# Pairing the 64-row remainder of a contraction in the two row halves of TensorE, and writing a bias to PSUM from ScalarE

## The chip, the cores and the metric

The kernel runs on one core of a Trainium2 chip. The metric is device time in microseconds (us) of one execution, the median of several. A profile's "span", from the first to the last instruction, is 1.4 to 2.1 us shorter than that time. The "granted clock" is the share of its full clock that TensorE was given, as a mean over the run unless a stretch is named. PSUM is the memory, in banks, in which TensorE's matmuls add up their sums; an "eviction" is the instruction of another engine that reads a finished sum out of it. The profile names the engines PE (TensorE matmul), PEld (TensorE weight load), DVE (VectorE), ACT (ScalarE), POOL (GpSimd) and SP (SyncE, which issues transfers). "L525" is line 525 of the kernel that is profiled, so the same code has other line numbers in other kernels.

## The reference, cut to what matters

```python
g = sigmoid((x * gate_w).sum(-1, keepdims=True))      # x: 2048 rows, 640 features
a = ssm(x, ...)                                       # complex recurrence, then y = 2 Re(h C) + x * Dskip
h = gelu(x @ w1 + b1)                                 # 640 -> 1728 features
b = h @ w2 + b2                                       # 1728 -> 640
out = g * a + (1 - g) * b
```

1728 = 13 x 128 + 64. The second linear layer, `h @ w2 + b2`, contracts over 13 full blocks of 128 features and a remainder of 64. The change is about that remainder and about `b2`.

## The kernel before

The 2048 rows are worked off in four chunks of 512 rows (four row tiles of 128). For each chunk there are four kinds of matmul work: `ssm` (input of the recurrence), `ff1` (first linear layer, with GELU on ScalarE), `fin_b` (second linear layer) and `fin_a` (output of the recurrence, C matrix). Their order is:

```python
    # ... ff1(0) ...
    ssm(0); ff1(1); ssm(1)
    for ks in range(KS):
        fold(ks)                 # scale the C matrix once, on ScalarE and VectorE
    fin_b(0); fin_a(0)
    ssm(2); ff1(2); fin_b(1); fin_a(1)
    ssm(3); ff1(3); fin_b(2); fin_a(2)
    fin_b(3); fin_a(3)           # (cut: gates, loads)
```

The second linear layer, and the scaling of C:

```python
    def fin_b(c):
        for a in range(TPC):                               # 4 row tiles (cut: ti and lo, the tile's number and first row)
            gb = fwork.tile([P, D], F32, name="gb")
            if a >= TPC - 2:
                seed(c * TPC + a - (TPC - 2))              # VectorE writes x * Dskip to PSUM for fin_a
            for d0, d1 in HALVES:                          # (0, 320), (320, 640)
                p = bank()
                for kf in range(KF):                       # 14: 13 full blocks and the remainder
                    m = P if kf < KF - 1 else F_LAST + 1   # 65 rows: 64 features and a row of ones for b2
                    nc.tensor.matmul(p[:, 0:d1 - d0], lhsT=gel[c][:m, kf, lo:lo + P], rhs=w2_sb[:m, kf, d0:d1],
                                     start=(kf == 0), stop=(kf == KF - 1))
                nc.scalar.activation(out=gb[:, d0:d1], in_=p[:, 0:d1 - d0], func=ACT.Identity, scale=gcol[:, 1, ti:ti + 1])

    def fold(ks):
        t1 = fwork.tile([P, D], F32, name="gb")
        t2 = fwork.tile([P, D], F32, name="gb")
        # ScalarE: t1 = CT_im * n2im ; t2 = CT_re * n2im
        # VectorE: CT_re = CT_re * c2re + t1 ; CT_im = CT_im * n2re + t2
```

In the timelines below, each engine starts its matmuls or evictions in the order in which the kernel issues them (ScalarE at the end of `ff1(2)`: L271 at 108.79, L295 at 109.46, L297 at 109.74). With `start=True` the first matmul of a group replaces what the bank held, so `fin_b` needs no value from another engine in its banks before it begins, and the trace of before has no wait of TensorE at its line, L525.

## Time and profile before

| | before |
|---|---|
| device time, median of 3 | 217.63 us (217.43 to 217.79) |
| span of the profiled run | 216.2 us |
| TensorE / VectorE / ScalarE busy | 98% / 88% / 42% |
| `fin_b` per chunk | 15.25 us, 112 matmuls of 320 columns, 136 ns each |

First the busy table of the page (engine, busy us, share of the span, instructions).

```profile
PE 211.9 (98%) x1368; PEld 128.2 (59%) x1368; DVE 189.8 (88%) x393; ACT 91.7 (42%) x156; POOL 1.6 (1%) x12
```

Then the chain of waits, in order of time (start us, length us, what, how many). This is the work that ended last, followed back from the end. From 22.5 us to the last matmul it is all matmuls; five of its pieces are shown: L267 is `ff1`, L525 `fin_b`, L544 `fin_a`.

```profile
57.81 15.25 PE bank L525 x112
73.06 10.87 PE bank L544 x80
94.72 14.03 PE bank L267 x65
109.36 15.24 PE bank L525 x112
202.27 10.91 PE bank L544 x90
```

Two unit costs can be read from it. 65 matmuls of 512 columns in 14.03 us make 215.8 ns each, 112 of 320 columns in 15.25 us make 136 ns each. A matmul's own duration in the profile is longer (299 ns for 320 columns) than the 136 ns from one start to the next, so the records of neighbours overlap: use this pitch, not the duration.

The timeline where `ff1(2)` ends and `fin_b(1)` begins (start us, length us, engine, line, operation). L292 is the small tile of the last 64 GELU features.

```profile
108.58 0.78 PE L292 MATMUL bank<-w1b,xT 128*128 128x65 bf16 x20
108.79 0.69 ACT L271 ACTIVATE gel<-bank,colB 128x512 bf16<-128x512 f32 x1 [0.39 <-PE bank L267]
109.20 0.57 PE L525 MATMUL bank<-w_sb,gel 128*128 128x320 bf16 x3
109.46 0.38 ACT L295 ACTIVATE gelN<-bank 128x256 bf16<-128x256 f32 x1
109.74 0.17 ACT L297 ACTIVATE gz<-bank 128x4 f32<-128x4 f32 x1
```

TensorE starts `fin_b` at 109.20, while ScalarE still has three evictions ahead of it. TensorE does not wait for them: the list of waits has only this one of TensorE, near the start of the kernel.

```profile
PE bank L196 <- DVE halfpi L191: 1.2, 1, 1.2
```

The first and the last VectorE instruction of the folding of C:

```profile
59.91 0.88 DVE L403 SCALAR_TENSOR_TENSOR CT_re<-CT_re,c2re,gb 128x640 bf16<-128x640 bf16 x1 [0.56 <-ACT gb L399]
67.08 0.88 DVE L403 SCALAR_TENSOR_TENSOR CT_im<-CT_im,n2re,gb 128x640 bf16<-128x640 bf16 x1
```

C is ready at 68 us, and `fin_a(0)` starts at 72.9.

### The profile page before, as it was taken

The numbers are of one execution on the slowest core, as the hardware profiler recorded it, in microseconds if no ns is written. First come the engines' busy times: TensorE is split into PE (matmuls) and PEld (weight loads), VectorE is DVE, ScalarE is ACT, GpSimd is POOL, SyncE is SP. The second block draws the span as 40 slices with busy tenths as digits, with TensorE's granted clock in tenths as the row PEclk, the third lists the DMA queues.
The fourth block names the chain that finished last, engine by engine and source line by source line (L and its number), as shares of the span: only waits on it lengthen the run. The fifth ranks groups of instructions, "written<-read, shape, count | busy, mean of one in ns | idle before, by whom it ended". The sixth has DMA issues, their size and how long they took to land.

```text
span 216.2 us, 3470 instructions
## 1 busy us (share of the span) xinstructions
PE 211.9 (98%) x1368; PEld 128.2 (59%) x1368; DVE 189.8 (88%) x393; ACT 91.7 (42%) x156; POOL 1.6 (1%) x12
## 2 busy tenths in 40 slices
PE   7999999999999999999999999999999999999994
PEld 3855444454577775444477777444457777777773
DVE  3889999999999899999999999999999999961152
ACT  3689456675696101556642200456662210022100
POOL 2000000000000000000000000000000000000000
PEclk9999999999999999999999999999999999999999
DMA  5999999995000042000010006100001000100011
GB/s 174 255 224 199 226 214 369 175 246 103 3 0 0 0 141 106 0 0 3 0 24 3 0 0 200 45 2 0 0 3 24 0 3 30 61 30 3 2 61 61
DMA packets 32339, 16.16 MB, mean 75 GB/s; under 512 B 25091, under 2 KB 32324, under 8 KB 32324
## 3 DMA queue, kind: packets, MB, share of 16 engines
q1 hardware_dynamic: 32114, 15.91, 30.2%
q8 instruction: 10, 0.16, 0.3%
q10 hardware_dynamic: 210, 0.04, 0.1%
q14 instruction: 5, 0.04, 0.1%
HBM read 7.24 MB, written 2.62 MB: 46 GB/s over the span
## 4 chain that ended last, share of the span: by engine, by line
PE 88%; SPq 5%; DMA 5%; issue 0%; DVE 0%
PE bank L525 28%; PE bank L544 20%; PE bank L478 20%; PE bank L267 19%; DMA BT_im<-in_A_B_im_dram 3%; SPq L139 3%; DMA xn<-in_A_x_dram 1%; SPq L127 1%; SPq L125 1%; PE bank L292 1%; SPq L124 0%; SPq L138 0%; DVE ot L549 0%
## 5 line engine op out<-in xcount | busy, mean ns | idle before, releaser
L525 PE MATMUL bank<-w_sb,gel 128*128 128x320 bf16 x448 | 61.6, 299 | 0.0
L525 PEld LDWEIGHTS <-gel 128*128 128x128 bf16 x448 | 43.6, 98 | 17.2
L481 ACT ACTIVATE bu<-bank 128x512 bf16<-128x512 f32 x40 | 23.9, 597 | 41.7 <-PE bank L478 41.7
L271 ACT ACTIVATE gel<-bank,colB 128x512 bf16<-128x512 f32 x52 | 34.6, 693 | 15.1 <-PE bank L267 14.8
L544 PEld LDWEIGHTS <-hs 128*128 128x128 bf16 x330 | 31.8, 98 | 11.9
L434 DVE TENSOR_TENSOR_SCAN g<-r_c,carry,v 128x512 bf16<-128x512 f32 x30 | 37.2, 1270 | 0.0
L528 ACT ACTIVATE gb<-bank,gcol 128x320 f32<-128x320 f32 x32 | 16.5, 527 | 48.2 <-PE bank L525 46.6
L267 PE MATMUL bank<-xT,w1b 128*128 128x512 bf16 x140 | 31.0, 379 | 0.0
L267 PE MATMUL bank<-xT,w1a 128*128 128x512 bf16 (+1 forms) x150 | 27.6, 344 | 0.0
L544 PE MATMUL bank<-CT_im,hs 128*128 128x320 bf16 (+2 forms) x165 | 27.1, 295 | 0.0
L544 PE MATMUL bank<-CT_re,hs 128*128 128x320 bf16 (+2 forms) x165 | 27.1, 295 | 0.0
L549 DVE SCALAR_TENSOR_TENSOR ot<-bank,gcol,gb 128x320 bf16<-128x320 f32 (+2 forms) x33 | 17.3, 533 | 9.5 <-PE bank L544 9.3
L478 PE MATMUL bank<-xT,BT_im 128*128 128x512 bf16 x100 | 24.9, 379 | 0.1
L478 PE MATMUL bank<-xT,BT_re 128*128 128x512 bf16 x100 | 24.8, 379 | 0.0
L267 PEld LDWEIGHTS <-w1b 128*128 128x128 bf16 x140 | 13.6, 98 | 16.3 <-DMA w1b<-in_B_w_dram 0.3
L267 PEld LDWEIGHTS <-w1a 128*128 128x128 bf16 x150 | 14.9, 100 | 11.7
L511 DVE TENSOR_TENSOR bank<-xn,Dbc 128x320 f32<-128x320 bf16 (+2 forms) x33 | 14.3, 483 | 5.8 <-ACT gb L528 5.8
L478 PEld LDWEIGHTS <-BT_im 128*128 128x128 bf16 x100 | 9.7, 98 | 12.2 <-DMA BT_im<-in_A_B_im_dram 0.6
L478 PEld LDWEIGHTS <-BT_re 128*128 128x128 bf16 x100 | 9.7, 98 | 11.0
L415 DVE TENSOR_TENSOR v<-wa,wb 128x512 bf16<-128x512 bf16 x40 | 15.2, 421 | 0.7
L415 DVE TENSOR_TENSOR wa<-TCOS,g 128x1024 bf16<-128x1024 bf16 x20 | 13.7, 686 | 0.1
L415 DVE TENSOR_TENSOR wb<-TSIN,g 128x1024 bf16<-128x1024 bf16 x20 | 13.7, 684 | 0.0
(98 smaller groups left out, 130.7 us busy)
## 6 DMA issues: line engine op xcount, KB each, us to landing
out_dram<-ot SPq DMA_DIRECT2D x15, 160.0 KB, 1.8
w_sb<-in_B_w_dram SPq DMA_DIRECT2D x1, 2080.0 KB
xn<-in_A_x_dram SPq DMA_DIRECT2D x3, 640.0 KB, 4.9
w1b<-in_B_w_dram SPq DMA_DIRECT2D x5, 240.0 KB, 4.2
w1a<-in_B_w_dram SPq DMA_DIRECT2D x5, 192.0 KB, 3.5
xn<-in_A_x_dram SPq DMA_DIRECT2D x2, 320.0 KB
Dbc<-in_A_Dskip_dram SPq DMA_DIRECT2D x1, 160.0 KB
out_dram<-ot SPq DMA_DIRECT2D x1, 128.0 KB
```

The source lines that it names most:

```text
L139: nc.sync.dma_start_transpose(out=BT_re[:], in_=A_B_re[:, :])
L267: nc.tensor.matmul(p[:, t0:t1], lhsT=w, rhs=xT[c][:, kd, t0:t1], start=(kd == 0), stop=(kd == KD - 1))
L271: nc.scalar.activation(out=gel[c][:, kf, :], in_=p[:, :], func=ACT.Gelu_apprx_tanh, bias=b1_c[:, kf:kf + 1])
L415: nc.vector.tensor_tensor(out=o, in0=a, in1=b, op=op)
L434: nc.vector.tensor_tensor_scan(s["g"][:, ri, :], r_c[:, ks:ks + 1].to_broadcast([P, CH]), s["v"][:, ri, :], init, ALU.mult, ALU.add)
L478: nc.tensor.matmul(p[:], lhsT=BT[:, kd, ks * P:(ks + 1) * P], rhs=xT[c][:, kd, :], start=(kd == 0), stop=(kd == KD - 1))
L481: nc.scalar.activation(out=bu[:, ri, :], in_=p[:], func=ACT.Identity)
L511: dve_now(ck.pe, 0.45, lambda: nc.vector.tensor_tensor(out=p[:, 0:d1 - d0], in0=xn[c][:, a, d0:d1], in1=Dbc[:, d0:d1], op=ALU.mult))
L525: nc.tensor.matmul(p[:, 0:d1 - d0], lhsT=gel[c][:m, kf, lo:lo + P], rhs=w2_sb[:m, kf, d0:d1], start=(kf == 0), stop=(kf == KF - 1))
L528: nc.scalar.activation(out=gb[:, d0:d1], in_=p[:, 0:d1 - d0], func=ACT.Identity, scale=gcol[:, 1, ti:ti + 1])
L544: nc.tensor.matmul(p[:, 0:d1 - d0], lhsT=hs[c][:, j, lo:lo + P], rhs=CT[:, j % KS, d0:d1], start=False, stop=(j == 2 * KS - 1), skip_group ...
L549: nc.vector.scalar_tensor_tensor(out=ot[:, d0:d1], in0=p[:, 0:d1 - d0], scalar=gcol[:, 0, ti:ti + 1], in1=gbs[ti][:, d0:d1], op0=ALU.mult, ...
```

## The change

The 65-row matmul takes as long as a 128-row one: `fin_b`, in which 8 of the 112 matmuls have 65 rows, runs at 136.2 ns a matmul, and `fin_a`, in which all have 128 rows and also 320 columns, at 10.87 us / 80 = 135.9 ns. The change packs the 64 remainder features of two row tiles above each other (partitions 0 to 63 and 64 to 127) and sends them through the upper and the lower half of TensorE's rows at the same time, all in one phase per chunk. That saves half of the remainder's column time. The ones row for `b2` no longer fits, so ScalarE writes `b2` to the banks beforehand and no matmul of the group clears. Tiles become 512 and 128 columns wide; the 128-column pieces of two row tiles share a bank. The five foldings of C, until now issued together before `fin_b(0)`, are spread among its tiles and get two scratch buffers of their own.

```diff
+    gelL = [const.tile([P, H, P], BF16, name=f"gelL{i}") for i in range(2)]
+    w2l = const.tile([P, D], BF16, name="w2l")        # the 64 rows of w2, twice
+    b2bc = const.tile([P, D], BF16, name="b2bc")      # b2 on every partition
@@ fold
-        t1 = fwork.tile([P, D], F32, name="gb")       # 5 buffers
-        t2 = fwork.tile([P, D], F32, name="gb")
+        t1 = fwork.tile([P, D], F32, name="ft", bufs=2)
+        t2 = fwork.tile([P, D], F32, name="ft", bufs=2)
@@ fin_b
+    MAIN, REST = (0, 512), (512, D)
+        def shared(d0, d1, n):                        # a bank that holds the bias
+            p = bank() ...
+            nc.scalar.activation(out=v, in_=src, func=ACT.Identity)
+        def full(p, col, a, d0, d1):                  # 13 full blocks, start=False
+        def half_rows():
+            for d0, d1 in (MAIN, REST):
+                for j in range(H):
+                    for h in range(2):
+                        p, col = (wide[h * H + j], 0) if d0 == 0 else (rest[h], j * dR)
+                        nc.tensor.matmul(p[:, col:col + d1 - d0], lhsT=gelL[c % 2][h * F_LAST:(h + 1) * F_LAST, j, :],
+                                         rhs=w2l[h * F_LAST:(h + 1) * F_LAST, d0:d1], start=False, stop=True, ...)
+        for h in range(2):
+            for j in range(H):
+                a = h * H + j
+                if h == 0:
+                    wide[a] = shared(*MAIN, 1)
+            # ... full tiles; after each one an entry of `between`; half_rows() after the first half
@@ order of the stages
-    for ks in range(KS):
-        fold(ks)
-    fin_b(0)
+    fin_b(0, [lambda: (fold(0), fold(1)), lambda: fold(2), lambda: fold(3), lambda: fold(4)])
```

(Cut: the smaller transpose of the remainder, evictions, buffer counts.)

More of the change, by code (lines that the diff above doesn't have):

```diff
@@ L28 @@
 TPC = CH // P
+H = TPC // 2
 HD = D // 2
@@ L69 @@
     work = ctx.enter_context(tc.tile_pool(name="work", bufs=2))
-    fwork = ctx.enter_context(tc.tile_pool(name="fwork", bufs=5))
+    fwork = ctx.enter_context(tc.tile_pool(name="fwork", bufs=4))
     def bank(dtype=F32):
@@ L80 @@
     w1b = [const.tile([P, n1b], BF16, name=f"w1b_{kd}") for kd in range(KD)]
-    w2_sb = const.tile([P, KF, D], BF16, name="w2_sb")
+    w2_sb = const.tile([P, KF - 1, D], BF16, name="w2_sb")
     BT_re = const.tile([P, KD, D], BF16, name="BT_re")
@@ L97 @@
     b1x = const.tile([P, F_LAST + 1], BF16, name="b1x")
-    gelN = [const.tile([P, TPC, P], BF16, name=f"gelN{i}") for i in range(2)]
+    gelN = [const.tile([P, H, P], BF16, name=f"gelN{i}") for i in range(2)]
+    gelL = [const.tile([P, H, P], BF16, name=f"gelL{i}") for i in range(2)]
+    w2l = const.tile([P, D], BF16, name="w2l")
+    b2bc = const.tile([P, D], BF16, name="b2bc")
     gz = const.tile([P, NT], F32, name="gz")
@@ L108 @@
     b1_c = colB[:, KS:NB]
-    H = TPC // 2
     def load_xn(c, a0=0, a1=TPC):
@@ L132 @@
     nc.gpsimd.memset(b1x[:, F_LAST:F_LAST + 1], 0.0)
-    for i in range(2):
-        nc.gpsimd.memset(gelN[i][:, :, F_LAST:P], 0.0)
-        nc.gpsimd.memset(gelN[i][:, :, F_LAST:F_LAST + 1], 1.0)
     nc.scalar.dma_start(out=prmB[KS:NB, :], in_=B_b1[0:(KF - 1) * P].rearrange("(j p) -> j p", p=P))
@@ L144 @@
     nc.sync.dma_start(out=w2_sb[:, 0:KF - 1, :], in_=B_w2[0:(KF - 1) * P, :].rearrange("(kf p) d -> p kf d", p=P))
-    nc.sync.dma_start(out=w2_sb[:F_LAST, KF - 1, :], in_=B_w2[(KF - 1) * P:F, :])
-    nc.sync.dma_start(out=w2_sb[F_LAST:F_LAST + 1, KF - 1, :], in_=B_b2.rearrange("(o d) -> o d", o=1))
+    for h in range(2):
+        nc.sync.dma_start(out=w2l[h * F_LAST:(h + 1) * F_LAST, :], in_=B_w2[(KF - 1) * P:F, :])
+    nc.sync.dma_start(out=b2bc[:], in_=B_b2.rearrange("(o d) -> o d", o=1).to_broadcast([P, D]))
     nc.sync.dma_start(out=Dbc[:], in_=A_Dskip.rearrange("(o d) -> o d", o=1).to_broadcast([P, D]))
@@ L227 @@
     nc.scalar.activation(out=r_c[:], in_=dtl[:], func=ACT.Exp)
-    scr = gelp.tile([P, KF * CH // 2], F32, name="gel")
+    scr = gelp.tile([P, (KF - 1) * CH // 2], F32, name="gel")
     HB = 2 * HC
@@ L294, in last_tile @@
                 pe(76)
-        nc.scalar.activation(out=gelN[c % 2][:, :, 0:F_LAST], in_=pv[:, :, 0:F_LAST], func=ACT.Gelu_apprx_tanh)
+        nc.scalar.activation(out=gelN[c % 2][:].rearrange("p j (h n) -> p h j n", h=2),
+                             in_=pv[:, :, 0:F_LAST].rearrange("p (h j) n -> p h j n", h=2), func=ACT.Gelu_apprx_tanh)
         act(0.45)
@@ L298, in last_tile @@
         act(0.2)
-        nc.sync.dma_start_transpose(out=gel[c][:, KF - 1, :].rearrange("p (a t) -> p a t", a=TPC),
-                                    in_=gelN[c % 2][:].rearrange("p a n -> p (a n)"))
+        nc.sync.dma_start_transpose(out=gelL[c % 2][:], in_=gelN[c % 2][:].rearrange("p a n -> p (a n)"))
     def ff1(c, k0=0):
@@ L314, in gel_tile @@
     def gel_tile(c):
-        gel[c] = gelp.tile([P, KF, CH], BF16, name="gel")
+        gel[c] = gelp.tile([P, KF - 1, CH], BF16, name="gel")
     gel_tile(0)
@@ L512, in seed @@
             seeded[ti].append(p)
-    def fin_b(c):
-        for a in range(TPC):
-            ti = c * TPC + a
-            lo = a * P
-            gb = fwork.tile([P, D], F32, name="gb")
-            if a >= TPC - 2:
-                seed(c * TPC + a - (TPC - 2))
-            for d0, d1 in HALVES:
-                p = bank()
-                for kf in range(KF):
-                    m = P if kf < KF - 1 else F_LAST + 1
-                    nc.tensor.matmul(p[:, 0:d1 - d0], lhsT=gel[c][:m, kf, lo:lo + P], rhs=w2_sb[:m, kf, d0:d1],
-                                     start=(kf == 0), stop=(kf == KF - 1))
-                    pe(d1 - d0)
-                nc.scalar.activation(out=gb[:, d0:d1], in_=p[:, 0:d1 - d0], func=ACT.Identity, scale=gcol[:, 1, ti:ti + 1])
-                act(0.5)
-            gbs[ti] = gb
+    MAIN, REST = (0, 512), (512, D)
@@ new lines, in fin_b, with out_of @@
+    def fin_b(c, between=()):
+        between = list(between)
+        wide, rest = [None] * TPC, [None] * H
+        def shared(d0, d1, n):
+            p = bank()
+            v = p[:, 0:n * (d1 - d0)]
+            src = b2bc[:, d0:d1]
+            if n > 1:
+                v = v.rearrange("p (j d) -> p j d", j=n)
+                src = src.rearrange("p (o d) -> p o d", o=1).to_broadcast([P, n, d1 - d0])
+            nc.scalar.activation(out=v, in_=src, func=ACT.Identity)
+            act(0.6 if n == 1 else 0.4)
+            return p
+        def full(p, col, a, d0, d1):
+            for kf in range(KF - 1):
+                nc.tensor.matmul(p[:, col:col + d1 - d0], lhsT=gel[c][:, kf, a * P:(a + 1) * P], rhs=w2_sb[:, kf, d0:d1],
+                                 start=False, stop=False, skip_group_check=True)
+                pe(d1 - d0)
+        def out_of(p, col, a, d0, d1):
+            ti = c * TPC + a
+            if gbs[ti] is None:
+                gbs[ti] = fwork.tile([P, D], F32, name="gb")
+            nc.scalar.activation(out=gbs[ti][:, d0:d1], in_=p[:, col:col + d1 - d0], func=ACT.Identity, scale=gcol[:, 1, ti:ti + 1])
+            act(0.7 if d1 - d0 > 320 else 0.4)
+        def half_rows():
+            dR = REST[1] - REST[0]
+            for d0, d1 in (MAIN, REST):
[3 more added lines that the diff above has]
+                        nc.tensor.matmul(p[:, col:col + d1 - d0], lhsT=gelL[c % 2][h * F_LAST:(h + 1) * F_LAST, j, :],
+                                         rhs=w2l[h * F_LAST:(h + 1) * F_LAST, d0:d1], start=False, stop=True, skip_group_check=True)
+                    pe(d1 - d0)
+            ck.pe += 0.2
+        for h in range(2):
+            for j in range(H):
+                a = h * H + j
+                if h == 0:
+                    wide[a] = shared(*MAIN, 1)
+            if h == 0:
+                rest[0] = shared(*REST, H)
+                wide[H] = shared(*MAIN, 1)
+            for j in range(H):
+                a = h * H + j
+                full(wide[a], 0, a, *MAIN)
+                if h == 0 and j == 0:
+                    for a2 in range(H + 1, TPC):
+                        wide[a2] = shared(*MAIN, 1)
+                    rest[1] = shared(*REST, H)
+                if h == 1:
+                    out_of(wide[a], 0, a, *MAIN)
+                    seed(c * TPC + j)
+                if between:
+                    between.pop(0)()
+                let_out(ck.pe)
+            for j in range(H):
+                full(rest[h], j * P, h * H + j, *REST)
+            if h == 0:
+                half_rows()
+                for j in range(H):
+                    out_of(wide[j], 0, j, *MAIN)
+            for j in range(H):
+                out_of(rest[h], j * P, h * H + j, *REST)
@@ L536, in fin_a @@
             lo = a * P
-            ot = fwork.tile([P, D], BF16, name="ot", bufs=3)
+            ot = fwork.tile([P, D], BF16, name="ot", bufs=2)
             if a < TPC - 2:
```

## The prediction

> **What bounds the kernel now.** TensorE. The page's busy table gives it 212 of 216.2 us, the chain of waits 88% of the span, and from 22.5 us to the end that chain is unbroken matmul. VectorE is at 88%, ScalarE at 42%. Time moves only if matmul work shrinks or TensorE is made to wait.
>
> **What the change saves.** From the chain, the second linear layer takes 15.25 us per chunk: 112 matmuls of 320 columns, 136 ns each. Streams of 512 columns run at 215.8 ns (14.03 us for 65), and the final tile (90 matmuls in 10.91 us) leaves 56 ns for 128 columns. After: 52 x 215.8 + 52 x 55.8 = 14.12 us, plus the half-row phase, 0.54 us if each pair runs at once: 0.58 us less per chunk, 2.3 us in all. Narrow tiles cost nothing extra: the 65-column matmuls already run at 30 ns with their own weight loads. The Trainium skill ("TensorE: Matmul & The Clock Gate", Part 3) says matmuls in different row groups overlap, about 4 ns apart; no instruction of this trace shows it. The skill ("TensorEngine Tiling (Array Packing)", Key Properties) says switching tiling mode drains TensorE; I estimate 0.1 to 0.4 us per chunk for both switches, 1 us in all.
>
> **What it adds on the critical path.**
> 1. *The bias write gates the first matmul.* Before, the layer began with a clearing matmul and waited for nothing. Now its first matmul waits for a ScalarE write, queued behind the last evictions of the stage before. In the timeline, at chunk 0 ScalarE is free at 58.34 us; a 512-column ACTIVATE takes 0.60 us; the first matmul can start near 58.95 instead of 57.65. At chunk 1 the queue is GELU, 64-feature GELU (0.38), gate tanh (done 109.91); the bias is there at 110.45, and TensorE wanted it at 109.20. Chunk 2 is the same (160.74 to 162.0). Chunk 3 follows output matmuls in which ScalarE idles. Three waits of 1.3 us: +3.9 us.
> 2. *Folding C, chunk 0.* Folds are now spread among the tiles with two scratch buffers, so ScalarE and VectorE alternate (about 2.5 us per fold instead of 1.6), and VectorE's order puts the remaining chunk-0 scan work, a seed pair, a scan and part of the next rotation ahead of folds 3 and 4. Before, VectorE finished folding at 68 us, 5 us ahead of need. Adding its measured durations in the new order (fold 0.80, rotation 0.60, scan 1.17, seed 0.43), fold 4's first half ends near 76.6 us; TensorE wants it at 74.4. Estimated stall +2.2 us.
>
> The six bias writes per chunk (3 us) sit otherwise in ScalarE's idle time.
>
> **Sum.** -2.3 + 1.0 + 3.9 + 2.2 = +4.8 us: **222.4 us**, 8 in 10 between 219.6 and 224.6. Faster by over 2%: 0.03; within 2%: 0.39; slower by over 2%: 0.58.
>
> **What would show each step right.** TensorE's waits: three of about 1.3 us on the bias writes before the first matmuls of chunks 0, 1 and 2, none in chunk 3; one of about 2 us in the first output tile of chunk 0, released by a VectorE fold. Streams of 512 and 128 columns at 216 and 56 ns. In the half-row phase the second matmul of a pair starts almost with the first; a phase takes 0.5 us plus some tenths of switching.
>
> **What would make it wrong.** Pairs that don't overlap (+2 us); a far dearer switch; a bias write that gets in earlier than I read; folds that VectorE reaches sooner, so that the fold stall is zero and the total lies within 2%.

## The result

| | before | after |
|---|---|---|
| device time, median of 6 | 217.68 us (217.26 to 218.07) | 222.50 us (222.16 to 224.60) |
| ratio | | 1.0241 (1.0202 to 1.0280) |

A ratio is the mean time of one kernel's runs over that of the other's in the same rounds, so it is not quite the ratio of the medians. The change made the kernel 2.4% slower.

The profiled execution is the slowest of the six (224.6 us, span 222.5, granted clock 0.992). Four of the six have a granted clock of 1.000 and spans of 220.4 to 220.7; the other two have 0.992 and spans of 222.5 and 221.9. That difference is explained below.

The busy table after:

```profile
PE 211.1 (95%) x1349; PEld 118.1 (53%) x1368; DVE 190.4 (86%) x393; ACT 101.8 (46%) x180; POOL 1.0 (0%) x8
```

Two of the entries that have TensorE as the waiting engine, from the list of waits (who waited for whom: us in total, times, longest us). L533 is the second layer, L597 `fin_a`. Before, neither existed (see above).

```profile
PE bank L533 <- ACT bank L527: 3.3, 3, 1.2
PE bank L597 <- DVE CT_re L403: 2.2, 1, 2.2
```

**The bias waits.** The timeline after, at the same place as shown of before. The chunk-1 bias is the first part of the two L527 writes, and stands behind L271, L295 and L298 in ScalarE's order.

```profile
113.55 0.77 PE L292 MATMUL bank<-w1b,xT 128*128 128x65 bf16 x20
113.75 0.69 ACT L271 ACTIVATE gel<-bank,colB 128x512 bf16<-128x512 f32 x1 [0.39 <-PE bank L267]
114.41 0.38 ACT L295 ACTIVATE gelN<-bank 128x256 bf16<-128x256 f32 x1
114.69 0.17 ACT L298 ACTIVATE gz<-bank 128x4 f32<-128x4 f32 x1
114.74 1.12 ACT L527 ACTIVATE bank<-b2bc 128x512 f32<-128x512 bf16 x2
115.40 0.81 PE L533 MATMUL bank<-w_sb,gel 128*128 128x512 bf16 x3 [1.08 <-ACT bank L527]
```

From the start of L292 to the start of `fin_b` were 0.62 us before and are 1.85 us now: TensorE loses 1.23 us. (The bracket shows less, 1.08, because the idle time is counted from the modelled end of the last matmul, which lies after the start of its successor in a stream.) Chunk 2 loses 1.24 us in the same way, chunk 0 1.34 us behind `ssm(1)`, chunk 3 nothing.

**The fold stall.** TensorE in chunk 0, then VectorE at the end of the same stretch:

```profile
58.95 7.22 PE L533 MATMUL bank<-w_sb,gel 128*128 128x512 bf16 x51 [1.18 <-ACT bank L527]
66.10 0.72 PE L550 MATMUL bank<-w2l,gelL 64*128 64x512 bf16 x8
66.75 7.24 PE L533 MATMUL bank<-w_sb,gel 128*128 128x512 bf16 x51
73.83 0.71 PE L597 MATMUL bank<-CT_re,hs 128*128 128x320 bf16 x4
76.74 0.41 PE L597 MATMUL bank<-CT_re,hs 128*128 128x320 bf16 x1 [2.20 <-DVE CT_re L403]
```

```profile
74.63 1.28 DVE L434 TENSOR_TENSOR_SCAN g<-r_c,carry,v 128x512 bf16<-128x512 f32 x1
75.82 0.86 DVE L403 SCALAR_TENSOR_TENSOR CT_re<-CT_re,c2re,ft 128x640 bf16<-128x640 bf16 x1
76.60 0.88 DVE L403 SCALAR_TENSOR_TENSOR CT_im<-CT_im,n2re,ft 128x640 bf16<-128x640 bf16 x1
```

Two earlier lines of VectorE, the folds of the second and third block of C, each of which it could only begin after a wait for ScalarE's scratch tile `ft`:

```profile
65.19 0.89 DVE L403 SCALAR_TENSOR_TENSOR CT_re<-CT_re,c2re,ft 128x640 bf16<-128x640 bf16 x1 [0.96 <-ACT ft L399]
67.83 0.89 DVE L403 SCALAR_TENSOR_TENSOR CT_re<-CT_re,c2re,ft 128x640 bf16<-128x640 bf16 x1 [0.96 <-ACT ft L399]
```

`fin_a(0)` runs four matmuls at 73.83 and then needs the fifth block of C. At 136 ns each the fifth matmul was due at 74.37; it starts at 76.74, right after VectorE's fold of that block ends at 76.68. The stall is 2.37 us. VectorE did a scan of 1.2 us just before the fold; it was never idle between 67.83 and 77.39, and between the third fold and the fifth it had 4.8 us of other work (2.8 us before the fourth, 2.0 us after it). Both the order and the two scratch buffers made it late. An estimate from these lines: without the two waits of 0.96 us the last fold would have ended near 74.8, still 0.4 us late; with the waits but without the other work, at the pitch of 2.64 us, near 74.0, in time. So the order alone seems enough to mend it, the buffers alone not quite. Neither was run alone.

**The gain.** `fin_b` takes 73.83 - 58.95 = 14.88 us from its first matmul to the first of the next stage, against 15.25 before, and 14.88 or 14.89 in the other three chunks. That is 0.37 us per chunk, 1.5 us in all.

**The clock.** Granted clock and work of TensorE in three stretches after the stall (stretch, its length, then for each engine busy us and the instructions that it touched, then the granted clock of TensorE as a share of full speed, DMA share and GB/s):

```profile
76.70:77.00 0.30, 0.26 (x2) 0.16 (x2) 0.30 (x1) 0.00 (x0) 0.00 (x0) 0.65 0.00 0
77.00:79.50 2.50, 2.50 (x11) 1.46 (x10) 1.84 (x4) 0.00 (x0) 0.00 (x0) 0.50 0.00 0
80.20:80.40 0.20, 0.20 (x3) 0.16 (x2) 0.00 (x0) 0.00 (x0) 0.00 (x0) 0.99 0.00 0
```

From about 76.8 to 80.2 us, some 3.4 us, the clock is halved, just after the stall. The 76 matmuls of `fin_a(0)` that follow the stall take 11.99 us until the next stage starts at 88.73; at 136 ns they would take 10.34. This costs the profiled run 1.65 us more, and half clock for 3.4 of 222.5 us makes a mean of 0.992, which is the mean of both longer runs. The second of them has no kept trace; that its clock fell at the same place is inferred.

**The account of the profiled run.** 1.34 + 1.23 + 1.24 (bias waits) + 2.37 (fold) + 1.65 (clock) - 1.47 (gain) = 6.36 us. The span grew by 222.5 - 216.2 = 6.3 us. Without the clock term the account gives 4.7 us; the four runs at full clock have a mean span of 220.6 us, 4.4 us over the profile of before.

### The profile page after: what moved, and what is told of

The parts are those of the page before. It is cut to its first block, busy times and chain, and to the rows that moved or that the text cites. A ratio compares the mean times of both kernels' runs of the same rounds, so it can differ in the third digit from the quotient of the medians. Undisturbed runs are those within 1.5% of the kernel's fastest.

```text
span 222.5 us, 3478 instructions
## 1 busy us (share of the span) xinstructions
PE 211.1 (95%) x1349; PEld 118.1 (53%) x1368; DVE 190.4 (86%) x393; ACT 101.8 (46%) x180; POOL 1.0 (0%) x8
## 4 chain that ended last, share of the span: by engine, by line
PE 78%; SPq 5%; ACT 5%; DMA 4%; DVE 4%; issue 2%
PE bank L597 20%; PE bank L533 19%; PE bank L478 19%; PE bank L267 19%; DMA BT_im<-in_A_B_im_dram 3%; SPq L138 3%; ACT bank L527 2%; DVE CT_re L403 2%; DMA xn<-in_A_x_dram 1%; ACT ft L397 1%; ACT ft L399 1%; SPq L129 1%; SPq L127 1%; PE bank L550 1%; DVE CT_im L403 1%
## 5 line engine op out<-in xcount | busy, mean ns | idle before, releaser
L533 PE MATMUL bank<-w_sb,gel 128*128 128x128 bf16 (+1 forms) x408 | 57.2, 297 | 3.9 <-ACT bank L527 3.3
L533 PEld LDWEIGHTS <-gel 128*128 128x128 bf16 x416 | 32.3, 98 | 29.0 <-issue 3.8
L271 ACT ACTIVATE gel<-bank,colB 128x512 bf16<-128x512 f32 x52 | 34.6, 693 | 15.3 <-PE bank L267 15.0
L597 PEld LDWEIGHTS <-hs 128*128 128x128 bf16 x330 | 32.3, 100 | 14.9 <-issue 2.4
L541 ACT ACTIVATE gb<-bank,gcol 128x512 f32<-128x512 f32 (+1 forms) x32 | 15.1, 525 | 34.2 <-PE bank L550 20.0
L597 PE MATMUL bank<-CT_re,hs 128*128 128x320 bf16 (+2 forms) x165 | 28.1, 301 | 2.2 <-DVE CT_re L403 2.2
L597 PE MATMUL bank<-CT_im,hs 128*128 128x320 bf16 (+2 forms) x165 | 28.1, 303 | 0.0
L267 PE MATMUL bank<-xT,w1a 128*128 128x512 bf16 (+1 forms) x147 | 26.8, 336 | 0.5 <-DMA xT<-in_A_x_dram 0.4
L267 PEld LDWEIGHTS <-w1a 128*128 128x128 bf16 x150 | 14.4, 98 | 11.9 <-issue 0.5
L527 ACT ACTIVATE bank<-b2bc 128x512 f32<-128x512 bf16 (+1 forms) x24 | 11.5, 527 | 5.3 <-DVE ot L602 5.3
```

The costliest lines, as they stand in the source:

```text
L267: nc.tensor.matmul(p[:, t0:t1], lhsT=w, rhs=xT[c][:, kd, t0:t1], start=(kd == 0), stop=(kd == KD - 1))
L271: nc.scalar.activation(out=gel[c][:, kf, :], in_=p[:, :], func=ACT.Gelu_apprx_tanh, bias=b1_c[:, kf:kf + 1])
L527: nc.scalar.activation(out=v, in_=src, func=ACT.Identity)
L533: nc.tensor.matmul(p[:, col:col + d1 - d0], lhsT=gel[c][:, kf, a * P:(a + 1) * P], rhs=w2_sb[:, kf, d0:d1], start=False, stop=False, skip_ ...
L541: nc.scalar.activation(out=gbs[ti][:, d0:d1], in_=p[:, col:col + d1 - d0], func=ACT.Identity, scale=gcol[:, 1, ti:ti + 1])
L597: nc.tensor.matmul(p[:, 0:d1 - d0], lhsT=hs[c][:, j, lo:lo + P], rhs=CT[:, j % KS, d0:d1], start=False, stop=(j == 2 * KS - 1), skip_group ...
```

## The experiments

The theory: the row halves work and give 1.5 us; three ScalarE bias writes and one VectorE fold, which the change put ahead of TensorE, cost 6.2 us. The rival: the new tile shapes and the half-row phase themselves cost the time (pairs that don't overlap, a dear change of mode, narrow matmuls that wait for their weights).

The first four ran on one chip; the kernel before ran 11 times beside them, median 217.84 us.

### e1: the folds issued together, bias writes left alone

```diff
-        t1 = fwork.tile([P, D], F32, name="ft", bufs=2)
-        t2 = fwork.tile([P, D], F32, name="ft", bufs=2)
+        t1 = fwork.tile([P, D], F32, name="gb")          # one pool of 6 for folds and outputs
+        t2 = fwork.tile([P, D], F32, name="gb")
-    fin_b(0, [lambda: (fold(0), fold(1)), lambda: fold(2), lambda: fold(3), lambda: fold(4)])
+    fin_b(0, [lambda: [fold(ks) for ks in range(KS)]])
```

> The changed kernel with all five folds issued together after the first tile, with six shared buffers, bias writes left as they are. Theory (three bias waits of 1.3 us, one fold stall of 2.4 us, plus a clock dip after that stall in some runs): the fold stall and the dip go, granted clock 1.00 in every run, 222.4 - 2.4 = 220.0 us, that is 1.1% over before; the bias waits stay at 1.2 to 1.3 us each. Rival (the new tiles and the half-row phase cost the time): no change, 222.4 us.

Measured: 220.05 us, ratio 1.0111 (1.0091 to 1.0130), correct. The clock was 0.998 or more in all six runs. TensorE's wait for ScalarE is still there (3.3 us in three, as after), and `fin_a(0)` starts without a break:

```profile
58.73 7.22 PE L533 MATMUL bank<-w_sb,gel 128*128 128x512 bf16 x51 [1.18 <-ACT bank L527]
73.61 0.84 PE L597 MATMUL bank<-CT_re,hs 128*128 128x320 bf16 x5
```

The fold stall was real, and the order and buffers of the folds were its cause. As the repair changes the order and the number of scratch buffers together, it doesn't tell which of the two mattered more (the estimate above says the order).

### e2: the first bias write moved ahead, folds left alone

```diff
+    def bias_early(c):
+        early[c] = bank()
+        nc.scalar.activation(out=early[c][:, 0:512], in_=b2bc[:, 0:512], func=ACT.Identity)
@@ ff1(c): before the matmuls of its last full tile
+            if c >= 2 and kf == KF - 2:
+                bias_early(c - 1)
@@ ssm(c): before the matmuls of its last bank
+                if c == 1 and ks == KS - 1 and ri == 1:
+                    bias_early(0)
@@ fin_b
-                    wide[a] = shared(*MAIN, 1)
+                    wide[a] = early.pop(c) if a == 0 and c in early else shared(*MAIN, 1)
```

> The changed kernel with the first bias write of chunks 0, 1 and 2 moved ahead of the last evictions of the stage before; folds left as they are. Theory: the three bias waits vanish (-3.9 us), but the second layer of chunk 0 then ends 1.3 us sooner while the folds move up only about 0.5 us, so the fold stall grows by about 0.8 us: 219.3 us, and still a dip of the clock in some runs. If the waits merely added up: 218.5 us. Rival (tiles and phase): 222.4 us.

Measured: 220.66 us, ratio 1.0120 (1.0087 to 1.0152), correct. The three bias waits are gone from the list of waits. By starts, nothing is left of them at chunks 1 and 2 (0.61 us from L292 to `fin_b`), but at chunk 0 `fin_b` begins 11.06 us after `ssm(1)`, against 10.79 before and 12.13 in the changed kernel: 0.27 us is left. The fold stall grew:

```profile
72.72 0.71 PE L608 MATMUL bank<-CT_re,hs 128*128 128x320 bf16 x4
76.19 0.30 PE L608 MATMUL bank<-CT_re,hs 128*128 128x320 bf16 x1 [2.77 <-DVE CT_re L412]
```

By the same reckoning as above (due at 72.72 + 0.54 = 73.26) it is 2.93 us instead of 2.37. Three of the six runs had a clock of 0.992 and a mean span of 219.6 us, the other three 1.000 and 217.9 us. The median of 220.66 lies between the two groups and is no good measure; the three runs at full clock (219.41, 219.81, 220.09) fit the expected 219.3. The expectation named the dip but put no size on it, so as a median it missed by 1.4 us.

### e3: both repairs

> Both repairs. Theory: only the gain is left, 4 chunks x (15.25 - 14.88) = 1.5 us: 216.1 us, 0.7% faster than before, TensorE without waits after the start. Rival (tiles and phase cost time): at or above before, 217.6 us or more.

Measured: 216.49 us (216.31 to 216.59), ratio 0.9938 (0.9924 to 0.9951), correct; clock 0.999 or more in every run. The list of waits has none of TensorE on a bias write or a fold. But the chain of waits still runs through the first bias write, L306, which ends just before `fin_b(0)` (L544) starts:

```profile
57.05 0.60 ACT bank L306
57.70 3.61 PE bank L544 x16
```

`fin_b(0)` begins 11.05 us after `ssm(1)`, 0.26 us more than before, so the early write at chunk 0 is not quite early enough and the expected "without waits" was missed by that. The kernel beats both others: 0.6% less than before (1.35 us in the medians), 2.7% less than the changed kernel.

The four kernels give the value of each repair, in mean spans of runs at full clock:

| | folds as changed | folds together |
|---|---|---|
| bias writes as changed | 220.6 (after, 4 runs) | 218.4 (e1) |
| first bias write early | 217.9 (e2, 3 runs) | 214.7 (e3) |

The bias repair is worth 2.7 us with the fold stall in place and 3.7 us without it. In chunk 0 the bias wait and the fold chain overlap in part: starting `fin_b(0)` 1.1 us sooner (57.84 instead of 58.95) only moved the fifth matmul of `fin_a(0)` from 76.74 to 76.19.

### e6: only the 512 and 128 wide tiles, in the kernel before

```diff
-            for d0, d1 in HALVES:
+            for d0, d1 in ((0, 512), (512, D)):
```

> The kernel before with only its second-layer tiles cut at 512 instead of 320 (14 matmuls deep as before, clearing first matmul, no bias write, no row halves). Theory: 14 x (215.8 + 55.8) = 3.80 us per row tile against 28 x 136.1 = 3.81 us, so 217.6 us within noise (0.1 us less at most). Rival (narrow tiles are costly): if each 128-column matmul took 80 ns instead of 56, 56 x 4 x 0.024 = +5.4 us, 223 us.

Measured: 217.69 us, ratio 1.0004 (0.9976 to 1.0032). In its trace `fin_b(0)` takes 15.25 us (57.94 to 73.19), as before. The tile shapes cost nothing, and they give nothing. The result of this kernel is wrong (relative error 0.46). The likely cause, argued and not tested: the Trainium skill ("PSUM — Partial Sum Buffer", The four PSUM rules) says a group's first matmul clears the accumulate marks of the whole bank and sets them again only for the columns it writes. After a 128-column group, VectorE's 320-column seed for `fin_a` would then be overwritten in 192 columns instead of added to. The changed kernel has no clearing matmul in `fin_b`; e1, e2 and e3, which share that `fin_b`, passed the comparison with the reference. The time stands, as every instruction was still run.

### e3 again, e4 and e5: what the half-row phase costs

The last three ran together on one chip (before: 217.76 us, 11 runs). Both wrong-result kernels start from e3. The comparison with the reference passed them as correct, presumably because 64 of 1728 features weigh too little for its tolerance; they are not usable kernels. For the same reason the pass of e1 to e3 does not show that their half-row sums are right.

> The repaired kernel again, as the base for the two wrong-result kernels of this call, on one chip: 216.5 us, the half-row phase 0.65 us per chunk from start to start, and 14.88 us from the first matmul of the second layer to the first after it.

Measured: 216.36 us, ratio 0.9946 (0.9925 to 0.9968). Chunk 0 of TensorE's timeline:

```profile
57.18 7.22 PE L544 MATMUL bank<-w_sb,gel 128*128 128x512 bf16 x51
64.33 0.72 PE L561 MATMUL bank<-w2l,gelL 64*128 64x512 bf16 x8
64.98 7.24 PE L544 MATMUL bank<-w_sb,gel 128*128 128x512 bf16 x51
72.06 0.84 PE L608 MATMUL bank<-CT_re,hs 128*128 128x320 bf16 x5
```

e4 takes both matmuls of a pair from the first row half:

```diff
-  lhsT=gelL[c % 2][h * F_LAST:(h + 1) * F_LAST, j, :],  rhs=w2l[h * F_LAST:(h + 1) * F_LAST, d0:d1]
+  lhsT=gelL[c % 2][0:F_LAST, j, :],                     rhs=w2l[0:F_LAST, d0:d1]
```

> The repaired kernel, but both matmuls of each pair take their 64 rows from the first row half (wrong result on purpose; same count, sizes, banks and mode switches). Theory (pairs run at once in different row halves): each pair now takes its turn, the phase grows from 0.65 to about 1.2 us, 4 x 0.54 = +2.2 us, 218.7 us. Rival (the two matmuls of a pair were never concurrent, and the gain came from elsewhere): no change.

Measured: 218.59 us, ratio 1.0049 (1.0026 to 1.0071): 2.2 us over e3. The phase lasts 66.02 - 64.83 = 1.19 us:

```profile
64.83 1.26 PE L561 MATMUL bank<-w2l,gelL 64*128 64x512 bf16 x8
66.02 7.24 PE L544 MATMUL bank<-w_sb,gel 128*128 128x512 bf16 x51
```

The overlap can also be seen directly, by counting the matmuls of the phase that are under way in short stretches (stretch, length, PE busy and count, PEld busy and count, clock). First the changed kernel, then e4, each some 0.02 and 0.28 us into the phase.

```profile
66.11:66.13 0.02, 0.02 (x2) 0.02 (x4) 1.00 0.00 0
66.37:66.39 0.02, 0.02 (x4) 0.02 (x2) 1.00 0.00 0
```

```profile
64.84:64.86 0.02, 0.02 (x1) 0.02 (x2) 1.00 0.00 0
65.10:65.12 0.02, 0.02 (x2) 0.02 (x1) 1.00 0.00 0
```

In the changed kernel the count goes up in twos: both matmuls of a pair are under way at once, and four where the next pair has begun before the first has drained. In e4 it goes up by one. Stretches of 2 ns put the second matmul of the first two pairs 2 to 4 ns behind the first, close to the 4 ns that the prediction cited.

e5 replaces each pair by one matmul over all 128 rows, which streams the same columns as a perfectly overlapped pair, without a change of tiling mode:

```diff
-                    for h in range(2):
+                    for h in range(1):
-  lhsT=gelL[c % 2][h * F_LAST:(h + 1) * F_LAST, j, :],  rhs=w2l[h * F_LAST:(h + 1) * F_LAST, d0:d1]
+  lhsT=gelL[c % 2][:, j, :],                            rhs=w2l[:, d0:d1]
```

> The repaired kernel, but each pair replaced by one matmul over all 128 rows into the first of its two banks (wrong result on purpose; same columns streamed as a perfectly overlapped pair, no change of tiling mode). Theory: what goes is the switching cost, 14.88 - 14.12 - 0.54 = 0.22 us per chunk, so 0.9 us less, 215.6 us. If switching into and out of the halves costs nothing: 216.5 us. If the prediction's 0.1 to 0.4 us were at its upper end: 214.9 us.

Measured: 215.40 us, ratio 0.9903 (0.9882 to 0.9925): 1.0 us under e3, 0.24 us per chunk. Its chunk 0:

```profile
57.42 7.22 PE L544 MATMUL bank<-w_sb,gel 128*128 128x512 bf16 x51
64.48 0.71 PE L561 MATMUL bank<-w2l,gelL 128*128 128x512 bf16 x4
65.03 7.23 PE L544 MATMUL bank<-w_sb,gel 128*128 128x512 bf16 x51
72.09 0.84 PE L608 MATMUL bank<-CT_re,hs 128*128 128x320 bf16 x5
```

From start to start, the stages ahead of, in and behind the phase take 7.15, 0.65 and 7.08 us in e3, and 7.06, 0.55 and 7.06 us in e5. So about 0.09 us go on the way into the row halves, 0.10 in the phase (which includes the way out) and 0.02 behind it, 0.21 us in all. This is the whole difference between e3 and e5: it holds the change of mode and whatever a pair in the halves costs more than one full matmul, which was not told apart.

## Why the prediction was right or wrong

The predicted 222.4 us met a median of 222.5, and the terms of the sum held one by one, each within 0.2 us, so the total is not a lucky sum of errors.

- *The saving, 2.3 us less 1.0 for switching.* Measured: 1.5 us net. Pairs overlap (e4: 2.2 us lost without it). Switching costs at most 0.21 us per chunk by the timeline and 0.24 by the times of e5, inside the 0.1 to 0.4 that was estimated. The prediction gives no working for that estimate; that it held is in part luck.
- *Narrow tiles cost nothing.* Right: e6 is 1.0004 of before, and its `fin_b(0)` also takes 15.25 us.
- *Three bias waits of 1.3 us, none in chunk 3.* Right: 1.34, 1.23 and 1.24 us; with the write moved ahead (e2) 0.27 us is left at chunk 0 and nothing at the other two.
- *A fold stall of 2.2 us, fold 4's first half done near 76.6 us.* Right, and by the named path: the first folds come at a pitch of 2.6 us (2.5 predicted), seeds and a scan stand ahead of the last one, which is done at 76.68, and the stall is 2.37 us. e1 takes it away.
- *Not foreseen: the clock.* In two of six runs the fold stall was followed by half clock, for 1.65 us more in the profiled one. The prediction's sum holds for the other four runs (222.16 to 222.65 us); the range of 219.6 to 224.6 took in the longest only at its edge.
- *Not said: the terms don't come off one by one.* The prediction added 1.3 us in chunk 0 and 2.2 us for the fold. As an account of the changed kernel this is right. As the worth of each repair it is not: mending the bias alone lengthened the fold stall by 0.56 us (e2).

## What to carry to other kernels

When an accumulator's start moves from a clearing matmul to a write by another engine, that write joins the engine's queue: issue it before the last evictions of the stage ahead. Here, issued after them, it made TensorE wait 1.2 to 1.3 us, three times. A trick that worked as meant (1.5 us) was lost four times over to two issue orders that it brought along, and moving one write in each of three chunks and one group of folds turned 2.4% slower into 0.6% faster. Count what a change puts ahead of the busiest engine, not only what it takes off it, and look at each run's clock before trusting a median when TensorE has a gap like the 2.2 us.

## What the Trainium skill lacked or had wrong

- "TensorE: Matmul & The Clock Gate" (Why this matters for your kernels) advises against idle gaps of more than about 3 us between matmul bursts. Here gaps of 2.2 us (idle, after) and 2.8 us (e2) were followed by half clock for about 3.4 us in the profiled runs (from 76.8 and from 77.0 us, 0.05 and 0.8 us after the gap ended), and the mean clock fell to 0.992 in 2 of 6 and 3 of 6 runs. Three gaps of 1.2 us per run left it at 0.998 or more in the six runs of e1. What decides in which runs it happens was not tested.
- The same page (Back-to-back issue gap) gives about 81 ns per 128-column and 131 ns per 512-column matmul as the sustained rate in a stream in which each has its own weight load. Here such streams ran at 55.8 ns (after: 26 matmuls from 128.83 to 130.28 us) and 215.8 ns (before: 65 in 14.03 us), which is the page's formula for an isolated gap.
- "TensorEngine Tiling (Array Packing)" (Key Properties) says that a change of tiling mode drains TensorE, but gives no size. Here into and out of two row halves together cost at most 0.21 to 0.24 us per phase (e3 against e5).
- "PSUM — Partial Sum Buffer" (Summary: rules for kernel authors) tells the reader to seed an accumulation from VectorE or ScalarE with 0 only. e1 to e3 seed it with the bias and with `x * Dskip`; the page's longer text says when this holds. e6 gave a relative error of 0.46, likely for want of it, which was not tested.
